# Attention and soft mixture of experts on one core: nine weight tiles in place of the last pair's tiles, another order at the end, and weight tiles that take the turned combine weights

## The chip, the core and the metric

The kernel runs on one core of a Trainium2 chip. The metric is the device time of one execution in microseconds. Several executions are timed and the median stands for the kernel; one further execution was profiled, and all rows of a profile in this document come from that one.

The core's engines work side by side, each through its own list of instructions: PE multiplies matrices (PEld is its weight load), DVE does vector work, ACT does activations and copies, POOL does further vector work, and SP issues the DMAs. They wait for each other by semaphores.

## The reference

An attention over 8 batches, 8 heads, 576 positions and 64 columns of a head is followed by a soft mixture of 8 experts with 4 slots each. All arrays are float32.

```python
# attention: q, k rotated (cos/sin by position), then for each head
scores = (1 / sqrt(D)) * matmul(q_rot, k_rot^T)
attn = exp(scores - max over keys); attn /= sum over keys + 1e-9
x = matmul(attn, v), written as N = 4608 rows of 512
# soft mixture of experts
logits = x @ phi                                  # 4608 x 32
d = exp(logits - max over rows); d /= sum over rows + 1e-9
slot_input = d.T @ x                              # 8 experts x 4 slots x 512
h = maximum(slot_input[e] @ w1[e], 0)             # 512 -> 1024
slot_out[e] = h @ w2[e]                           # 1024 -> 512
c = exp(logits - max over slots); c /= sum over slots + 1e-9
out = c @ slot_out                                # 4608 x 512
```

## The kernel before

**Attention.** The 64 heads are worked as 32 pairs; four pairs are a batch. A pair goes through these tasks: `load0`, `load1` bring q and k (L144); `spin` multiplies by cos and sin on POOL (L149, for pair 0 on DVE); `join` adds (L153); `high` and `low` split into two fp16 parts (L158, L162). The `m` units multiply one part and take row maxima on DVE (L184, L192); `t` units make the scores transposed (L229) and the exponentials on ACT (L230, tiles `a_t` and `a_rem`); `av` units multiply with v (L245, tile `v_in`); `o_out` copies the result to `xt` (L253). `add` sums exponential tiles on DVE into `c_t` (L260, L263), `total` adds them up on PE (L273) and `total_out` copies the sums to `s4` on ACT (L278). For most pairs the reciprocal sums then travel through DRAM (L284 to L304, tile `rb`) and POOL multiplies (L307). For the last two pairs `sums_turn` (L309) brings the sums from rows to columns on PE: five products with `fold`, a 0/1 tile of two columns, then two reciprocals that read PSUM (L316, L317); `sums_wide` (L326) spreads them, `norm_wide` (L332) multiplies. `logits` (L360), `natural` (L342, the transposes to `xn`) and the softmax over rows with a running maximum follow.

**Order.** PE, ACT, DVE, and in the attention SP and POOL too, run in the order in which the program writes the instructions. A table `WHEN` gives each task its place in a repeating beat. Ahead of the beat a start is written out: pair 0's work, the `fold` tile (L639, L641), 23 and 16 warm-up matmuls (`heat`, L630), pair 1's first tasks. After the beat the last pair's tasks are written out (L685 to L698), and then the slot inputs (L705 to L773).

**Weights.** The experts' weights come as 64 tiles of 512 KB, 32 of w1 and 32 of w2, through `load_w` (L477), all on SP's one queue in program order. The first 24 (pool `wp`) come during the attention. Others take memory that becomes free: `wa` and `wx` that of the q and k tiles, `wk` and `we` that of the fp16 parts, `wl` (L525, two tiles) that of `att` (`a_t`, `a_rem`, `c_t`) in `release_att`, `wb` (L767, two tiles) that of `xn`. The rest reuse `wp` tiles as FFN1 reads them out: seven issued ahead (`N_LEAD`), the others after FFN1's second group.

**The experts and the output.** FFN1 (L784) is four groups of 16 matmuls, FFN2 (L808) two halves `mh` of 16 steps of 4 matmuls. `c_turn(q)` turns a quarter of the combine weights: six transposes (`c_tr`, L448) of what `c_split` left in `csp` (an ACT copy L436 and a POOL subtraction L437), and six copies on ACT (`c_evac`, L459, L462) into `cst` and `crt`. There is one `csp`, so a split comes after the turn before it. Quarter 0 is turned between the slot inputs (L744 to L746), quarter 1 after the first FFN1 group (L858), the others where `TURNS` puts them, the last one inside the combine (L889). `gather` (L821) adds the experts' slot outputs from `so` (L812, L813); `combine` (L836, L837) multiplies and stores (L840, L843), nine stores for each half.

Of the kernel before, what the change touches and what calls it, by code (L numbers as in the profile page):

```python
# [7 lines left out]
F32 = mybir.dt.float32  # L8
F16 = mybir.dt.float16
F32R = mybir.dt.float32r  # L10
AF = mybir.ActivationFunctionType
ALU = mybir.AluOpType
AX = mybir.AxisListType
PSUM = bass.MemoryType.PSUM

B, H, S, D = 8, 8, 576, 64
HALF = D // 2
NP = H // 2
# [9 lines left out]
KB = S // D  # L28
N_W = 24
# [1 line left out]
N_WA = 5  # L31
N_WB = 2
N_WE = 3
N_WL = 2
N_X = 4
N_CS = 1
N_CE = 2
C_POOL = 4
LATE = (0, 2)
N_LEAD = 7  # L40
TURNS = (0, 0, 1, 0, 0, 0)
LEAD_STEPS = 2
STEPS = (1, 2, 2, 2, 2, 2, 2, 2, 1)
N_WARM = 23
N_CST = 4 - N_CE
RC = 12
PIECE = 4
WHEN = {
# [20 lines left out]
def attn_softmoe(ctx, tc, qk, v, phi, w1, w2, cs, ident, sel, seg, out):  # L69
    nc = tc.nc  # L70
    P = 128

    const = ctx.enter_context(tc.tile_pool(name="const", bufs=1))
    small = ctx.enter_context(tc.tile_pool(name="small", bufs=3))
    wp = ctx.enter_context(tc.tile_pool(name="wp", bufs=N_W))
# [2 lines left out]
    vals = ctx.enter_context(ExitStack())  # L78
    late = vals.enter_context(tc.tile_pool(name="late", bufs=2))
    trans = ctx.enter_context(ExitStack())  # L80
    att = trans.enter_context(tc.tile_pool(name="att", bufs=1))
    early = ctx.enter_context(ExitStack())
    stk = early.enter_context(tc.tile_pool(name="stk", bufs=4))
# [4 lines left out]
    ps_s = banks.enter_context(tc.tile_pool(name="ps_s", bufs=3, space=PSUM))  # L88
# [8 lines left out]
    id_sb = const.tile([P, P], F32, name="id_sb")  # L97
    phi_sb = const.tile([P, NP, NS], F32, name="phi_sb")
    sel_sb = const.tile([P, NS], F32, name="sel_sb")
    bits = const.tile([P, 5], F32, name="bits")  # L100
    ones, warm, tiny, fold = bits[:, 0:1], bits[:, 1:2], bits[:, 2:3], bits[:, 3:5]
    nc.vector.memset(ones, 1.0)
    lift = const.tile([P, P], F16, name="lift")
    nc.vector.memset(lift, 0.0)
# [59 lines left out]
    vts = {}  # L164

    def load_v(p):
        vts[p] = late.tile([P, KB, 2, D], F32, name="v_in")
        nc.sync.dma_start(out=vts[p], in_=v[p])

    nms = {}  # L170
# [1 line left out]
    def bank2():  # L172
        return ps_s.tile([P, 2, 512], F32, name="s_ps")
# [112 lines left out]
    rbs = {}  # L286
# [12 lines left out]

    def widen(p, eng):  # L300
        rd = sg.pop(p)
        rbs[p] = rb = late.tile([P, S], F32, name="rb", bufs=1)
        for h in range(2):
            eng.dma_start(out=rb[rows[h]], in_=rd[h:h + 1].broadcast_to([64, S]))  # L304

# [3 lines left out]
    def sums_turn(p):  # L309
        s4 = sg.pop(p)  # L310
        t = bank2()
        for j in range(5):
            w = P if j < 4 else 64
            nc.tensor.matmul(t[0:w, 0, 2 * j:2 * j + 2], lhsT=s4[:, P * j:P * j + w], rhs=fold, start=True, stop=True)
        rn = small.tile([P, RC], F32, name="rr", bufs=2)
        nc.vector.reciprocal(out=rn[:, 0:8], in_=t[:, 0, 0:8])  # L316
        nc.vector.reciprocal(out=rn[0:64, 8:10], in_=t[0:64, 0, 8:10])  # L317
        sg[p] = rn

    def sums_wide(p):  # L320
# [112 lines left out]
    def c_split(q):  # L433
        csp = c_tiles[0][2][q % N_CS]
        cb = cn_sb[:, 2 * q:2 * q + 2]
        nc.scalar.copy(out=csp[:, :, :, 0, :], in_=cb)  # L436
        (nc.gpsimd if q < C_POOL else nc.vector).tensor_tensor(  # L437
            out=csp[:, :, :, 1, :], in0=cb, in1=csp[:, :, :, 0, :], op=ALU.subtract)
# [3 lines left out]
    def c_tr(q):  # L442
        csp = c_tiles[0][2][q % N_CS]
        turning[q] = ps_s.tile([P, 2, 512], F32, name="s_ps")
        for b in range(2):
            for j in (0, 2, 4):
                w = P if j < 4 else 64
                nc.tensor.transpose(turning[q][0:w, b, 64 * j:64 * j + P],  # L448
                                    csp[:, b, j:min(j + 2, 5)].rearrange("p j a n -> p (j a n)").bitcast(F32), id_sb)

    def c_evac(q, both=False):
        cst, crt, _ = c_tiles[0]
        t = turning.pop(q)
        copies = (nc.scalar.copy, nc.vector.tensor_copy)
        for d in range(2):
            dst = slice(64 * d, 64 * d + 64)
            copy = copies[d * both]
            for s in range(2):
                copy(out=cst[q][dst, :, s::2, :],  # L459
                     in_=t[64 * s:64 * s + 64, :, 0:256].rearrange("p b (u x) -> p b u x", u=2))  # L460
                yield
            copy(out=crt[dst, 2 * q:2 * q + 2, :], in_=t[0:64, :, 320:384])  # L462
            yield

    def c_turn(q):
        c_tr(q)
        list(c_evac(q))

    w_tiles = {}
    extra = []  # L470
    later = []
    swap = list(range(4, 5 + N_CST))
    order = [n for n in range(8 * E) if n not in swap]
# [3 lines left out]
    def load_w(pool, bufs, tag="w_exp"):  # L477
        n = order[len(w_tiles)]
        layer, rest = divmod(n, 4 * E)
        if layer == 0:  # L480
            grp, f, ch, x = rest // 16, rest // 8 % 2, rest // 4 % 2, rest % 4
            src = w1[4 * grp + x].rearrange("(c p) f -> p c f", p=P)[:, 2 * ch:2 * ch + 2, 512 * f:512 * f + 512]
            wt = pool.tile([P, 2, 512], F32, name=tag, bufs=bufs)
        else:
            mh, grp, fh, x = rest // 16, rest // 8 % 2, rest // 4 % 2, rest % 4
            src = w2[4 * grp + x].rearrange("(c p) m -> p c m", p=P)[:, 4 * fh:4 * fh + 4, 256 * mh:256 * mh + 256]
            wt = pool.tile([P, 4, 256], F32, name=tag, bufs=bufs)
        nc.sync.dma_start(out=wt, in_=src)
        w_tiles[n] = wt
# [22 lines left out]
    def release_att():  # L512
        trans.close()
        cp = ctx.enter_context(tc.tile_pool(name="cp", bufs=1, side="right", reuse_waits="tile"))
        cst = [cp.tile([P, 2, 4, P], F32R, name=f"cst{i}") for i in range(N_CE)]
        crt = cp.tile([P, B, 64], F32R, name="crt")
        csps = [cp.tile([P, 2, 5, 2, NS], F32R, name=f"csp{i}") for i in range(N_CS)]
        c_tiles.append((cst, crt, csps))
        extra.append([cp.tile([P, 2, 2, 256], F32R, name=f"so{i}") for i in range(2)])
        seg_in = cp.tile([P, 320], F32, name="seg_in")  # L520
        nc.sync.dma_start(out=seg_in, in_=seg)
        seg_sb = cp.tile([P, 320], F32R, name="seg_sb")
        nc.gpsimd.tensor_copy(out=seg_sb, in_=seg_in)
        c_tiles.append(seg_sb)
        wl = ctx.enter_context(tc.tile_pool(name="wl", bufs=N_WL, side="right", reuse_waits="tile"))  # L525
        for _ in range(N_WL):
            load_w(wl, N_WL)

# [107 lines left out]
    do("load1", 2)  # L636
    nc.sync.dma_start(out=phi_sb, in_=phi.rearrange("(c p) n -> p c n", p=P))
    nc.sync.dma_start(out=sel_sb, in_=sel)
    nc.vector.memset(fold, 0.0)  # L639
    for i in range(0, P, 32):  # L640
        nc.vector.tensor_copy(out=fold[i:i + 2], in_=id_sb[i:i + 2, i:i + 2])  # L641
    do("spin1", 1)
    do("spin0", 1)
    for j in range(4):
# [34 lines left out]
    p = NPAIR - 1  # L679
# [2 lines left out]
    while pending:  # L682
        step(p)
    release_stk()
    for name in ("add1", "add2", "av4", "av5", "av6", "av7", "av8", "o_out", "total", "total_out"):  # L685
        do(name, p)
    steady.close()
    release_att()
# [9 lines left out]
    natural_out([p], nc.vector.tensor_copy)  # L698
    vals.close()
    banks.close()  # L700
    ps_t = ctx.enter_context(tc.tile_pool(name="ps_t", bufs=3, space=PSUM))
    ps_a = ctx.enter_context(tc.tile_pool(name="ps_a", bufs=1, space=PSUM))
    ps_s = ctx.enter_context(tc.tile_pool(name="ps_s2", bufs=2, space=PSUM))

    eb = const.tile([P, P], F32, name="e_blk")  # L705
    e = const.tile([P, NS], F32, name="e_sel")
# [33 lines left out]
    for i in range(NP):  # L740
        nc.tensor.matmul(rp[32 * i:32 * i + 32], lhsT=dn[64:P, P + 32 * i:P + 32 * i + 32],
                         rhs=xn[64:P, 4, i * P:(i + 1) * P], start=True, stop=True, tile_position=(64, 32 * i))
    mains(1)
    c_tr(0)  # L744
    c_split(1)
    list(c_evac(0))  # L746
    next(stat)
    nc.gpsimd.tensor_scalar_mul(out=zs, in0=zacc[:, 1:2], scalar1=0.25)
    nc.gpsimd.tensor_tensor(out=zs, in0=zs, in1=zacc[:, 0:1], op=ALU.add)
# [25 lines left out]
    cst, crt, _ = c_tiles[0]  # L775
# [66 lines left out]
            for h in range(2):  # L842
                nc.sync.dma_start(out=of[h::2, 512:576, ms].rearrange("b p m -> p b m"), in_=ob[64 * h:64 * h + 64])  # L843

    turned, split = 2, 2

    def c_turns(n):
        nonlocal turned, split
        for _ in range(n):
            if turned < NP:  # L850
                c_turn(turned)
                turned += 1
            if split < min(turned + N_CS, NP):
                c_split(split)
                split += 1

    prev = (0, 0, ffn1(0, 0))
    c_turn(1)  # L858
    cst.extend(extra[1].tile([P, 2, 4, P], F32R, name="w_exp", bufs=N_CST) for _ in range(N_CE, B // 2))
    c_split(2)  # L860
    split = 3
    for grp, f in ((0, 1), (1, 0), (1, 1)):
        h = ffn1(grp, f)
        ffn1_turn(*prev)
        prev = (grp, f, h)
        if (grp, f) == (0, 1):
            list(c_soft_tasks(B - 1, ps_t.tile([P, 512], F32, name="t_ps")))
            while len(w_tiles) < 8 * E:
                load_w(wp, N_W)
        c_turns(TURNS[2 * grp + f - 1])  # L870
    sos = extra[3]
    steps = ffn2_steps(0, sos[0])
    for k in range(16):
        next(steps)
# [2 lines left out]
        if k == 8:  # L877
            c_turns(TURNS[3])
    steps = ffn2_steps(1, sos[1])
    c_turns(TURNS[4])  # L880
    sl0 = gather(0, sos[0])
    c_turns(TURNS[5])
    for _ in range(LEAD_STEPS):
# [61 lines left out]
```

## Time and profile before

| what | value |
|---|---|
| timed executions | 596.29, 599.23, 595.2 us; median 596.29 |
| the profiled execution | 591.94 us, of which the span of the records is 590.2 us |
| PE busy | 529.8 us, 90% of the span |
| DVE, ACT, POOL busy | 430.9, 330.1, 296.6 us |
| HBM read, written | 99.93 MB, 9.58 MB |
| mean granted clock of TensorE | 0.974 |
| first FFN1 matmul (L784) | at 518.75 us |
| first store issued (L840), last two (L843) | 556.23 us, from 581.45 us on |

A row of a view with a time in front gives start and duration in us, engine, line, operation, tile written and tiles read, shapes and the count of records; in brackets the idle time of the engine before it and what ended that. A float32 matmul leaves two records. A row of the waits gives who waited for whom, us in total, times and the longest.

### The profile page before, as it was taken

The numbers are of one execution on the slowest core, as the hardware profiler recorded it, in microseconds if no ns is written. First come the engines' busy times: TensorE is split into PE (matmuls) and PEld (weight loads), VectorE is DVE, ScalarE is ACT, GpSimd is POOL, SyncE is SP. The second block draws the span as 40 slices with busy tenths as digits, with TensorE's granted clock in tenths as the row PEclk, the third lists the DMA queues.
The fourth block names the chain that finished last, engine by engine and source line by source line (L and its number), as shares of the span: only waits on it lengthen the run. The fifth ranks groups of instructions, "written<-read, shape, count | busy, mean of one in ns | idle before, by whom it ended". The sixth has DMA issues, their size and how long they took to land.

```text
span 590.2 us, 23663 instructions
## 1 busy us (share of the span) xinstructions
PE 529.8 (90%) x10320; PEld 354.6 (60%) x10320; DVE 430.9 (73%) x644; ACT 330.1 (56%) x640; POOL 296.6 (50%) x332
## 2 busy tenths in 40 slices
PE   3569989999999999999899999999999999799870
PEld 2247667657666766667666766676667666445440
DVE  5789799789888897988878888887888742321341
ACT  2136656566757665666566666666656564453341
POOL 2756467466665655566567857657593011110000
PEclk9579999999999999999999999999999999999996
DMA  7244655555555555555655555555443246589998
GB/s 249 82 162 123 182 180 180 180 180 180 180 180 180 181 180 181 181 183 178 189 171 178 180 181 191 183 171 176 158 135 101 64 147 224 192 275 349 349 361 271
DMA packets 71735, 111.65 MB, mean 189 GB/s; under 512 B 20176, under 2 KB 47568, under 8 KB 71632
## 3 DMA queue, kind: packets, MB, share of 16 engines
q1 hardware_dynamic: 71618, 110.15, 58.0%
q8 instruction: 81, 1.33, 1.0%
q14 instruction: 22, 0.18, 0.1%
q10 hardware_dynamic: 14, 0.00, 0.0%
HBM read 99.93 MB, written 9.58 MB: 186 GB/s over the span
## 4 chain that ended last, share of the span: by engine, by line
PE 57%; DVE 15%; DMA 14%; ACT 4%; SPq 4%; issue 3%; POOL 0%; DVEq 0%; ACTq 0%; POOLq 0%
PE o_ps L245 15%; PE s_ps L229 15%; PE s_ps L273 7%; DMA rc<-s 5%; PE s_ps L182 5%; DVE nm L184 4%; DVE hl L162 4%; SPq L284 3%; DMA w_exp<-in_w 3%; PE s_ps L784 2%; DMA x_in<-in_qk 2%; PE s_ps L342 2%; DVE x_in L153 2%; DVE c_t L263 1%; PE s_ps L360 1%
## 5 line engine op out<-in xcount | busy, mean ns | idle before, releaser
L149 POOL TENSOR_TENSOR x_in<-x_in,cs_sb 128x288 f32<-128x288 f32 x248 | 221.1, 923 | 121.5 <-DMA x_in<-in_qk 116.3
L184 DVE TENSOR_REDUCE nm<-s_ps 128x2 f32<-128x576 f32 x256 | 182.3, 750 | 54.2 <-PE s_ps L182 54.0
L230 ACT ACTIVATE a_t<-s_ps 128x576 f32<-128x576 f32 x256 | 160.5, 649 | 86.9 <-PE s_ps L229 72.2
L229 PE MATMUL s_ps<-hl 64*64 64x288 f16 x3456 | 159.9, 286 | 6.7 <-ACT xn L351 5.0
L245 PE MATMUL o_ps<-a_t,v_in 64*64 64x288 f32 x2048 | 163.1, 406 | 0.6 <-ACT xt L253 0.3
L229 PEld LDWEIGHTS <-hl 64*64 64x64 f16 x3456 | 101.8, 107 | 42.8 <-issue 28.3
L182 PE MATMUL s_ps<-hl 64*64 64x288 f16 x1024 | 84.5, 296 | 18.4 <-DVE nm L184 14.4
L229 PE MATMUL s_ps<-peak,lift 64*64 64x288 f16 x1152 | 92.3, 284 | 1.5 <-DMA peak<-mr 1.2
L307 POOL TENSOR_TENSOR xt<-xt,rb 128x576 f32<-128x576 f32 x30 | 49.9, 1664 | 73.0 <-DMA rb<-r_row 73.0
L245 PEld LDWEIGHTS o_ps<-a_t,v_in 64*64 64x64 f32 x2048 | 73.1, 133 | 16.2 <-ACT xt L253 3.8
L182 PEld LDWEIGHTS <-hl 64*64 64x64 f16 x1024 | 45.6, 106 | 43.0 <-issue 26.5
L158 ACT CAST hl<-x_in 128x576 f16<-128x576 f32 (+1 forms) x66 | 43.0, 653 | 26.3 <-DVE x_in L153 24.6
L153 DVE TENSOR_TENSOR x_in<-x_in 128x1152 f32<-128x1152 f32 (+2 forms) x36 | 53.1, 1475 | 1.6 <-POOL x_in L149 1.4
L278 ACT ACTIVATE s<-s_ps,bits 128x576 f32<-128x576 f32 x32 | 23.7, 740 | 49.9 <-PE s_ps L273 29.8
L162 DVE TENSOR_TENSOR hl<-x_in,hl 128x1152 f16<-128x1152 f32 x32 | 46.6, 1458 | 1.8 <-ACT hl L158 1.8
L260 DVE TENSOR_TENSOR c_t<-a_t 128x1152 f32<-128x1152 f32 x32 | 47.1, 1472 | 0.0
L229 PEld LDWEIGHTS <-lift 64*64 64x64 f16 x1152 | 40.2, 107 | 4.6 <-issue 3.6
L273 PE MATMUL s_ps<-a_t,pick 128*32 128x288 f32 x384 | 36.7, 406 | 0.0
L253 ACT COPY xt<-o_ps 128x576 f32<-128x576 f32 x32 | 20.4, 638 | 14.0 <-PE o_ps L245 14.0
L837 DVE COPY w_exp<-t_ps 128x512 f32<-128x512 f32 x18 | 12.3, 691 | 18.5 <-PE t_ps L836 17.9
L192 DVE TENSOR_REDUCE nm<-s_ps 128x2 f32<-128x576 f32 x32 | 24.0, 751 | 1.9 <-PE s_ps L190 0.8
L263 DVE TENSOR_TENSOR c_t<-c_t,a_t 128x576 f32<-128x576 f32 x32 | 24.9, 778 | 0.1
(182 smaller groups left out, 552.1 us busy)
## 6 DMA issues: line engine op xcount, KB each, us to landing
x_in<-in_qk SPq DMA_DIRECT2D x62, 576.0 KB
w_exp<-in_w SPq DMA_DIRECT2D x63, 512.0 KB
v_in<-in_v SPq DMA_DIRECT2D x32, 576.0 KB
rb<-r_row SPq DMA_DIRECT2D x60, 144.0 KB
out<-w_exp SPq DMA_DIRECT2D x16, 512.0 KB
rc<-s SPq DMA_DIRECT2D x120, 4.5 KB
x_in<-in_qk SPq DMA_DIRECT2D x4, 288.0 KB
out<-w_exp SPq DMA_DIRECT2D x4, 256.0 KB
```

What stands on the lines that cost most here:

```text
L149: eng.tensor_tensor(out=x[:, :, c], in0=x[:, :, c], in1=cs_sb[:, :, c], op=ALU.mult)
L153: nc.vector.tensor_tensor(out=x[:, t, 0, c], in0=x[:, t, 0, c], in1=x[:, t, 1, c], op=ALU.add)
L158: nc.scalar.copy(out=halves[p][:, 1 + t, c], in_=loaded[p][:, t, 0, c])
L162: nc.vector.tensor_tensor(out=hl[:, 0:4:3], in0=x[:, :, 0], in1=hl[:, 1:3], op=ALU.subtract)
L182: nc.tensor.matmul(s[rows[c], h, 0:HC], lhsT=hl[rows[h], QH, at:at + D], rhs=hl[rows[h], KH, half[n]], start=True, stop=True)
L184: nc.vector.tensor_reduce(out=nms[p][:, n, j:8:4], in_=s[:, :, 0:HC], axis=AX.X, op=ALU.max, negate=True)
L229: nc.tensor.matmul(s[rows[h ^ n], n, 0:HC], lhsT=lhs, rhs=rhs, start=(i == 0), stop=(i == 3))
L230: nc.scalar.activation(out=weights_of(p, b).rearrange("p (n x) -> p n x", n=2), in_=s[:, :, 0:HC], func=AF.Exp, scale=SCALE)
L245: nc.tensor.matmul(o[rows[h], n, 0:HC], lhsT=vt[r, b, n], rhs=a[r, half[n]], start=(b == 0), stop=(b == KB - 1))
L260: nc.vector.tensor_tensor(out=cts[p], in0=ats[p, 0], in1=ats[p, 1], op=ALU.add)
L273: nc.tensor.matmul(s[32 * i:32 * i + 32, n, 0:HC], lhsT=pick[:, n:n + NS], rhs=parts[cut][:, half[n]], start=first, stop=last, tile_positi ...
L307: eng.tensor_tensor(out=xts[p], in0=xts[p], in1=rbs.pop(p), op=ALU.mult)
```

## The change

1. `wl` gets nine tiles instead of two. They take the place of `att` and of a new pool `vp`, which holds `v_in` (two tiles) and `rb` and closes together with `att`. Room on that side comes from `cst0`, `cst1` and the two `so` tiles, which leave the pool `cp`: all four turned combine weights and both `so` now lie in weight tiles that were read out (two in `wa`, the others in `wp`).
2. In the last pair `total` and `total_out` are written ahead of `av7`, `av8` and `o_out`.
3. `sums_turn` transposes with `id_sb` and adds on DVE (two reductions, two reciprocals in SBUF) in place of the products with `fold`. The tile `fold`, its memset and its four copies at the start are gone.
4. `c_tr(0)`, `c_split(1)` and the copies of quarter 0 are no longer ahead of FFN1, nor quarter 1 after its first group: quarter 0 is turned after FFN1's third group, quarter 1 after the fourth, quarter 2 inside FFN2's first half (after its ninth of 16 steps), quarter 3 inside the combine as before.
5. The three PSUM pools of the end get waits by tile.

At the end of SP's queue (`wk` is the load of `hx`, the next three are `we`, `seg_in` a small table) before:

```order
L488 DMA wk<-in_w 128x2x512
L488 DMA w_exp<-in_w 128x4x256 x3
L521 DMA seg_in<-in_seg 128x320
L488 DMA w_exp<-in_w 128x4x256 x2
L488 DMA w_exp_11381<-in_w 128x4x256
L488 DMA w_exp_11383<-in_w 128x4x256
L488 DMA w_exp<-in_w 128x4x256 x25
```

and now:

```order
L493 DMA wk<-in_w 128x2x512
L493 DMA w_exp<-in_w 128x4x256 x3
L525 DMA seg_in<-in_seg 128x320
L493 DMA w_exp<-in_w 128x4x256 x9
L493 DMA w_exp_11379<-in_w 128x4x256
L493 DMA w_exp_11381<-in_w 128x4x256
L493 DMA w_exp<-in_w 128x4x256 x18
```

Behind `seg_in` nine `wl` loads instead of two stand ahead of the two numbered `wb` loads; of the loads into `wp` tiles 18 are left of 25.

On PE from the last pair's `av` units to its sums (`s_11221`, now `s_11211`, is `s4`) before:

```order
L245 MATMUL o_ps<-a_t,v_in 64x288 x12
L245 MATMUL o_ps<-a_rem,v_in 64x288 x4
L273 MATMUL s_ps<-c_t,pick 32x288 x4
L273 MATMUL s_ps<-a_t,pick 32x288 x5
L273 MATMUL s_ps<-a_rem,pick 32x288
L273 MATMUL s_ps<-a_t,pick 32x288
L273 MATMUL s_ps<-a_rem,pick 32x288
L314 MATMUL s_ps<-bits,s_11221 128x2 x4
L314 MATMUL s_ps<-bits,s_11221 64x2
```

and now:

```order
L245 MATMUL o_ps<-a_t,v_in 64x288 x8
L273 MATMUL s_ps<-c_t,pick 32x288 x4
L273 MATMUL s_ps<-a_t,pick 32x288 x5
L273 MATMUL s_ps<-a_rem,pick 32x288
L273 MATMUL s_ps<-a_t,pick 32x288
L273 MATMUL s_ps<-a_rem,pick 32x288
L245 MATMUL o_ps<-a_t,v_in 64x288 x4
L245 MATMUL o_ps<-a_rem,v_in 64x288 x4
L315 MATMUL s_ps<-id_sb,s_11211 128x128 x4
L315 MATMUL s_ps<-id_sb,s_11211 64x128
```

Eight matmuls of `av7` and `av8` moved behind `total`; the turn is four transposes of 128 columns and one of 64.

On ACT in FFN1's second half and FFN2's first (L797 copies FFN1's turned result, L812 a slot output) before:

```order
L797 COPY wk<-t_ps 128x512
L459 CAST w_exp<-s_ps 64x4x128 x2
L462 CAST crt<-s_ps 64x128
L459 CAST w_exp<-s_ps 64x4x128 x2
L462 CAST crt<-s_ps 64x128
L436 CAST csp_11231<-cn_sb 128x10x32
L797 COPY wk<-t_ps 128x512
L812 CAST so_11232<-o_ps 128x256
L812 CAST so_11232<-s_ps 128x256
```

and now (L795 and L810 are these copies):

```order
L467 CAST crt<-s_ps 64x128
L441 CAST csp_11230<-cn_sb 128x10x32
L795 COPY wk<-t_ps 128x512
L810 CAST w_exp<-o_ps 128x256
L464 CAST w_exp<-s_ps 64x4x128 x2
L467 CAST crt<-s_ps 64x128
L464 CAST w_exp<-s_ps 64x4x128 x2
L467 CAST crt<-s_ps 64x128
L441 CAST csp_11230<-cn_sb 128x10x32
L810 CAST w_exp<-s_ps 128x256
```

Before, quarter 2's copies and the split after them stood ahead of FFN1's last turned copy, and the two slot-output copies followed each other; now quarter 1's copies stand in that place (their last rows are the first here), and quarter 2's copies and the last split stand between the two slot-output copies.

The diff, cut to its core:

```diff
-N_WL = 2
+N_WL = 9
-TURNS = (0, 0, 1, 0, 0, 0)
+TURNS = (0, 1, 1, 1, 0, 0)
-N_CST = 4 - N_CE
+N_CST = 2
...
+    vp = trans.enter_context(tc.tile_pool(name="vp", bufs=2))
     att = trans.enter_context(tc.tile_pool(name="att", bufs=1))
...
-        vts[p] = late.tile([P, KB, 2, D], F32, name="v_in")
+        vts[p] = vp.tile([P, KB, 2, D], F32, name="v_in")
...
-        rbs[p] = rb = late.tile([P, S], F32, name="rb", bufs=1)
+        rbs[p] = rb = vp.tile([P, S], F32, name="rb", bufs=1)
...
     def sums_turn(p):
         s4 = sg.pop(p)
         t = bank2()
+        rn = small.tile([P, RC], F32, name="rr", bufs=2)
         for j in range(5):
             w = P if j < 4 else 64
-            nc.tensor.matmul(t[0:w, 0, 2 * j:2 * j + 2], lhsT=s4[:, P * j:P * j + w], rhs=fold, start=True, stop=True)
-        rn = small.tile([P, RC], F32, name="rr", bufs=2)
-        nc.vector.reciprocal(out=rn[:, 0:8], in_=t[:, 0, 0:8])
-        nc.vector.reciprocal(out=rn[0:64, 8:10], in_=t[0:64, 0, 8:10])
+            nc.tensor.transpose(t[0:w, j // 4, P * (j % 4):P * (j % 4) + P], s4[:, P * j:P * j + w], id_sb)
+        for w, n in ((P, 4), (64, 1)):
+            k = 0 if n == 4 else 8
+            nc.vector.tensor_reduce(out=rn[0:w, k:k + 2 * n].rearrange("p (j h) -> p j h", h=2),
+                                    in_=t[0:w, k // 8, 0:P * n].rearrange("p (j i r) -> p j r i", i=4, r=32)[:, :, 0:2],
+                                    axis=AX.X, op=ALU.add)
+        nc.vector.reciprocal(out=rn[:, 0:8], in_=rn[:, 0:8])
+        nc.vector.reciprocal(out=rn[0:64, 8:10], in_=rn[0:64, 8:10])
...
-        cst = [cp.tile([P, 2, 4, P], F32R, name=f"cst{i}") for i in range(N_CE)]
+        cst = []
...
-        extra.append([cp.tile([P, 2, 2, 256], F32R, name=f"so{i}") for i in range(2)])
...
-    nc.vector.memset(fold, 0.0)
-    for i in range(0, P, 32):
-        nc.vector.tensor_copy(out=fold[i:i + 2], in_=id_sb[i:i + 2, i:i + 2])
...
-    for name in ("add1", "add2", "av4", "av5", "av6", "av7", "av8", "o_out", "total", "total_out"):
+    for name in ("add1", "add2", "av4", "av5", "av6", "total", "total_out", "av7", "av8", "o_out"):
...
-    c_tr(0)
-    c_split(1)
-    list(c_evac(0))
     next(stat)
...
-    turned, split = 2, 2
+    turned, split = 0, 1
...
     prev = (0, 0, ffn1(0, 0))
-    c_turn(1)
-    cst.extend(extra[1].tile([P, 2, 4, P], F32R, name="w_exp", bufs=N_CST) for _ in range(N_CE, B // 2))
-    c_split(2)
-    split = 3
+    cst.extend(extra[1].tile([P, 2, 4, P], F32R, name="w_exp", bufs=N_CST) for _ in range(N_CST))
...
             while len(w_tiles) < 8 * E:
                 load_w(wp, N_W)
+            cst.extend(wp.tile([P, 2, 4, P], F32R, name="w_exp", bufs=N_W) for _ in range(N_CST, NP))
+            sos = [wp.tile([P, 2, 2, 256], F32R, name="w_exp", bufs=N_W) for _ in range(2)]
...
-    sos = extra[3]
```

More of the change, by code (lines that the diff above doesn't have):

```diff
@@ L33 @@
 N_WE = 3
-N_WL = 2
+N_WL = 9
 N_X = 4
 N_CS = 1
-N_CE = 2
 C_POOL = 4
@@ L99, in attn_softmoe @@
     sel_sb = const.tile([P, NS], F32, name="sel_sb")
-    bits = const.tile([P, 5], F32, name="bits")
-    ones, warm, tiny, fold = bits[:, 0:1], bits[:, 1:2], bits[:, 2:3], bits[:, 3:5]
+    bits = const.tile([P, 3], F32, name="bits")
+    ones, warm, tiny = bits[:, 0:1], bits[:, 1:2], bits[:, 2:3]
     nc.vector.memset(ones, 1.0)
@@ L700, in attn_softmoe @@
     banks.close()
-    ps_t = ctx.enter_context(tc.tile_pool(name="ps_t", bufs=3, space=PSUM))
-    ps_a = ctx.enter_context(tc.tile_pool(name="ps_a", bufs=1, space=PSUM))
-    ps_s = ctx.enter_context(tc.tile_pool(name="ps_s2", bufs=2, space=PSUM))
+    ps_t = ctx.enter_context(tc.tile_pool(name="ps_t", bufs=3, reuse_waits="tile", space=PSUM))
+    ps_a = ctx.enter_context(tc.tile_pool(name="ps_a", bufs=1, reuse_waits="tile", space=PSUM))
+    ps_s = ctx.enter_context(tc.tile_pool(name="ps_s2", bufs=2, reuse_waits="tile", space=PSUM))
     eb = const.tile([P, P], F32, name="e_blk")
```

## The prediction

> **What bounds the kernel now.** The page's chain that ended last, read first, says who ends last over the whole span; the table of windows says it for single stages.
>
> ```profile
> PE 57%; DVE 15%; DMA 14%; ACT 4%; SPq 4%; issue 3%; POOL 0%; DVEq 0%; ACTq 0%; POOLq 0%
> 484.00:494.00 10.00, 9.67 (x224) 6.38 (x216) 3.25 (x6) 6.14 (x12) 0.60 (x2) 1.00 0.56 162
> 508.00:512.00 4.00, 2.83 (x46) 2.34 (x45) 1.06 (x4) 0.05 (x1) 1.31 (x2) 1.00 1.06 353
> 512.00:518.00 6.00, 4.54 (x56) 3.07 (x49) 4.62 (x15) 2.37 (x10) 1.62 (x6) 1.00 0.29 89
> 518.00:528.00 10.00, 9.61 (x84) 3.53 (x87) 1.68 (x3) 6.33 (x15) 1.46 (x2) 1.00 0.87 290
> 528.00:556.00 28.00, 26.54 (x304) 13.01 (x296) 7.18 (x13) 10.73 (x25) 1.78 (x3) 1.00 1.09 349
> 570.00:574.00 4.00, 3.40 (x20) 2.72 (x20) 2.83 (x5) 2.10 (x4) 0.00 (x0) 1.00 0.99 300
> 574.00:584.00 10.00, 2.20 (x12) 1.38 (x11) 2.77 (x4) 2.34 (x4) 0.00 (x0) 0.82 1.05 358
> 584.00:590.20 6.20, 0.00 (x0) 0.00 (x0) 0.00 (x0) 0.00 (x0) 0.00 (x0) 0.50 0.54 151
> ```
>
> The columns are the stretch, its length, the busy times of PE, PEld, DVE, ACT and POOL, the granted clock, the DMA share and GB/s. In the attention loop TensorE is busy for 9.67 of 10 us: there a us counts on PE alone. From 528 the DMA engines are full, at 349 GB/s. But between 512 and 528 they carry 89 and 290 GB/s. The waits and the chain of the end say what that hole costs.
>
> ```profile
> SPq L488 <- DVE xn L352: 5.8, 1, 5.8
> PE s_ps L808 <- DMA w_exp<-in_w: 2.6, 4, 0.9
> PE o_ps L808 <- DMA w_exp<-in_w: 0.9, 1, 0.9
> 554.78 8.55 DMA w_exp<-in_w
> 571.44 6.75 DMA out<-w_exp
> ```
>
> The load queue stood 5.8 us behind one wait (a weight tile that takes the place of xn). Later FFN2 stands 2.6 + 0.9 = 3.5 us for weights, the chain goes through a weight load of 8.55 us and then through an output store: the tail hangs on bytes.
>
> **The start.** The four copies into `fold` and its memset go. On DVE they stand between two instructions of the chain:
>
> ```profile
> 12.01 1.36 DVE L162 TENSOR_TENSOR hl<-x_in,hl 128x1152 f16<-128x1152 f32 x1 [0.50 <-ACT hl L158]
> 13.42 2.86 DVE L641 COPY bits<-id_sb 2x2 f32<-2x2 f32 x4
> 16.32 1.43 DVE L184 TENSOR_REDUCE nm<-s_ps 128x2 f32<-128x576 f32 x2
> 32.08 1.35 DVE L153 TENSOR_TENSOR x_in<-x_in 128x1152 f32<-128x1152 f32 x1
> 12.44 13.84 POOL L149 TENSOR_TENSOR x_in<-x_in,cs_sb 128x288 f32<-128x288 f32 x16 [10.17 <-DMA x_in<-in_qk]
> ```
>
> L184 can start when L162 ends, at 12.01 + 1.36 = 13.37 instead of 16.32: 2.95 us. What could take it back is POOL, whose 16 rotations end at 12.44 + 13.84 = 26.28; DVE joins the last of them, pair 2's, at L153, 32.08, which would move to 29.13: cover of 2.85 remains. The other taker is the clock.
>
> ```profile
> 26.00:28.00 2.00, 2.00 (x17) 1.20 (x19) 0.00 (x0) 0.67 (x1) 0.28 (x1) 0.64 0.00 0
> 34.00:36.00 2.00, 0.61 (x8) 0.37 (x9) 1.26 (x1) 1.79 (x4) 0.02 (x1) 0.57 1.00 408
> 40.00:42.00 2.00, 2.00 (x44) 1.68 (x40) 1.53 (x3) 0.65 (x1) 2.00 (x4) 0.72 0.28 113
> ```
>
> With half speed before and full speed after a switch, or the reverse, the means 0.64, 0.57 and 0.72 put the switches at 27.44 (up), 34.28 (down) and 41.12 (up), 6.84 apart. [...]
>
> [...]
>
> **Pair 30's sums.** This turn runs inside the dense loop, so its PE time counts.
>
> ```profile
> 494.00 1.26 PE L314 MATMUL s_ps<-bits,s 128*128 128x2 f32 x10
> 499.85 1.09 PE L342 MATMUL s_ps<-id_sb,xt 128*128 128x128 f32 x8
> 512.00 0.66 PE L342 MATMUL s_ps<-id_sb,xt 128*128 128x128 f32 x4
> ```
>
> The ten records of L314 take 1.26 us. Eight transposes take 1.09 and four 0.66, so one more costs 0.11 and five take 0.77: 0.5 us saved (bounds 0 and 0.5). The two new reductions on DVE are hidden: their reader comes two tasks later.
>
> **The end, up to FFN1.**
>
> ```profile
> 503.28 1.94 PE o_ps L245 x32
> 507.76 1.27 PE s_ps L314 x10
> 59.83 0.23 DVE L290 TENSOR_REDUCE rr<-rc 96x12 f32<-96x48 f32 x1 [0.35 <-DMA rc<-s]
> 516.30 0.81 PE s_ps L448 x6
> 516.78 0.59 DVE L736 SCALAR_TENSOR_TENSOR acc<-acc,al,s_ps 128x128 f32<-128x128 f32 x2
> 518.75 3.64 PE s_ps L784 x32
> ```
>
> The sums now go ahead of av7 and av8, half of L245's 1.94, 0.97; these fill PE while ACT copies the sums. The turn starts when they end, about 0.9 earlier. It takes 0.77 instead of 1.27, but two reductions stand before the reciprocals, 0.23 (L290) or a little less each, overlapped: net -0.2, bounds -0.5 and +0.2. Turning combine weights of quarter 0 (L448, 0.81) no longer stands before L762; since DVE's L736 ends only at 517.37 and the last matmuls of L762 need it, I count half of it, 0.4. FFN1 starts 0.9 + 0.2 + 0.4 = 1.5 us earlier (bounds 0.9 and 2.0). Waits by tile on the PSUM pools may add a tenth; I count 0.
>
> Against the reciprocals, which now read and write SBUF, the trace has the other ones, and a POOL instruction near them:
>
> ```profile
> L291 DVE RECIPROCAL rr<-rr x30: 223/224/225, 60.1 to 486.3; 96x12 f32<-96x12 f32 x30
> 508.13 0.86 POOL L437 TENSOR_TENSOR csp<-cn_sb,csp 128x320 fp32r<-128x320 f32 x1 [6.38 <-ACT csp L436]
> ```
>
> Thirty of them, all through the loop in which POOL rotates and normalises, stayed within 223 and 225 ns: no stall. [...]
>
> **The end, from FFN1.** Nine loads instead of two can issue when the last pair's tiles are dead, about 507. Their waits: av8 (PE) for the first, the last a_rem and c_t for the second, all done by then; behind them on SP stand only loads and stores. The two loads over xn and the seven over FFN1's tiles come after them in the queue: at 1.5 us each the nine keep SP busy to about 520, past the matmuls for which it stood. Seven more tiles of 0.524 MB at 349 GB/s are 7 x 1.50 = 10.5 us of transfer. The hole takes (349 - 89)/349 x 6 = 4.47 and (349 - 290)/349 x 10 = 1.69, so 6.16 us: it is filled, and every later byte moves 6.16 ahead.
>
> PE is the other limit. All three turns c_tr(0), (1), (2) now stand inside the FFN instead of two: +0.81. The tiles that now hold the turned weights and `so` were read by FFN1 matmuls that stand ahead of their first writers on PE: 0, and a late one would be rival B. ACT gets their copies:
>
> ```profile
> 536.66 1.17 ACT L459 CAST w_exp<-s_ps 64x512 fp32r<-64x512 f32 x2
> 539.57 0.46 ACT L436 CAST csp<-cn_sb 128x320 fp32r<-128x320 f32 x1
> 538.21 2.73 PE o_ps L808 x48
> 544.45 0.37 ACT L812 CAST so<-s_ps 128x256 fp32r<-128x256 f32 x1 [3.08 <-PE s_ps L808]
> 569.47 0.69 DVE L837 COPY w_exp<-t_ps 128x512 f32<-128x512 f32 x1 [1.08 <-PE t_ps L836]
> 570.52 10.82 SPq L840 DMA_DIRECT2D out<-w_exp  x8
> ```
>
> A turn's copies and the split after it hold ACT from 536.66 to 540.03, 3.4 us. After c_tr(2) the PE has 28 matmuls of L808 left, 56 records at 2.73/48, 3.2 us: the copy of `so` (L812) comes 0.2 late and the gather waits for it. The second half of FFN2 thus starts 1.5 - 0.81 - 0.2 = 0.5 earlier; without its 3.5 us of waiting for weights it ends 4.0 earlier. The second half's first store is ready by PE 4.0 earlier, while the bytes are 6.16 ahead. From 570 on 4 x 300 + 10 x 358 + 6.2 x 151 kB/us make 5.72 MB; stores not yet issued at 570.52 are 9 x 0.524 = 4.72: the queue then holds 1.0 MB, 2.8 us, which covers the 2.2 of lateness except for the time from issue to first byte. I let it lose about half: the end gains **5.0** (bounds 4.0 by PE, 6.16 by bytes).
>
> **Sum.** 2.95 + 0.5 + 5.0 = 8.45 us. The profiled execution of 591.94 (span 590.2) would take 583.5; the median shown is 596.29, 4.35 above it, and I keep that distance: 587.8 us. The likeliest case's own range is 585.5 to 590.5.
>
> **Rivals.**
> (A) The start's 2.95 is eaten, by POOL or by warm-up matmuls that fall in another phase of the clock: 5.5 us remain, 590.8. For it: PE at half speed in much of the first 41 us; against it: POOL's 26.28 lies before 29.13.
> (B) The end stays with PE and ACT: the three turns' copies delay FFN1's own copies and the gather by 2 us more, so that the end gains 2.5 us: 590.3. For it: 3.4 us of ACT per turn; against it: ACT is busy only 10.73 of 28 us in 528 to 556.
> (C) The change doesn't do what it says: the nine loads are freed late, after the last xt or xn, and the hole stays. Only the start, 0.5 and the 0.5 by which the second half starts earlier are left: 592.3. Against it: the tiles' last readers end before 508.
> (D) Slower: v_in, rb and the a_t tiles get other SBUF addresses, and the loop's reads meet conflicts in all 32 pairs. It cancels the gain from 8.45/32 = 0.26 us a pair; at 0.5 it gives 596.29 + 16 - 8.45 = 603.8.
>
> ```profile
> L245 PE MATMUL o_ps<-a_t,v_in x2048: 400/402/738, 38.0 to 504.3; 64*64 64x288 f32 x187
> ```
>
> Against it: these 2048 read two v_in buffers and four a_t buffers at different places, and minimum and median are 400 and 402 ns.
>
> **How the numbers follow.** Forecast 0.66, A 0.10, B 0.12, C 0.07, D 0.05. One per cent, about what a measurement tells from no change, is 5.96 us: faster means below 590.3. The forecast is nearly all faster; A and B lie about at the bound and are split; C is the same; D slower. That gives faster 0.75, same 0.20, slower 0.05. The range leaves out D and the far ends: 584.5 to 592.5.
>
> **What would show it.** Right: L184 starts near 13.4; DMA carries about 349 GB/s from 508 without a hole; FFN1 starts about 5 us earlier than 518.75; FFN2 waits for weights under 1 us; the last store lands about 8 earlier. Wrong: FFN1 early but the hole at 512 to 518 still there (C); a full DMA but gather and L812 late (B); pairs longer than before (D); a first dense matmul no earlier (A).

## The result and the profile after

The changed kernel takes 580.71 us in the median (578.42 to 581.86, four executions) where the kernel before took 597.41 on the same chip: ratio 0.9717, 95% interval 0.9669 to 0.9766. A second measurement, beside other experiments, gave 0.9791 (0.9742 to 0.984). Both say faster: 16.7 us between the first medians, 12.5 by the second ratio (14.6 between its medians, 596.58 and 582.0); the forecast was 8.45. Between the two profiled executions it is 591.94 to 580.32, 11.6 us; the spans are 590.2 and 578.5.

The start, in the chain of the changed kernel (start, length, engine, tile, line, count):

```profile
13.28 3.99 DVE nm L184 x6
34.10 1.18 PE s_ps L229 x15
490.55 0.70 PE s_ps L315 x5
```

The first row maximum starts at 13.28 instead of 16.32. The five transposes of pair 30 (L315) take 0.70 where L314 took 1.26. The table of windows at the end (columns as before):

```profile
504.00:508.00 4.00, 2.70 (x42) 2.08 (x42) 1.93 (x7) 0.24 (x2) 0.17 (x1) 1.00 1.02 337
508.00:512.00 4.00, 2.77 (x31) 1.24 (x31) 3.06 (x11) 1.38 (x8) 2.47 (x7) 1.00 1.09 352
512.00:518.00 6.00, 5.62 (x38) 2.07 (x41) 0.88 (x4) 0.00 (x0) 0.00 (x0) 0.72 1.09 348
518.00:528.00 10.00, 10.00 (x92) 3.74 (x88) 2.91 (x6) 2.10 (x6) 0.92 (x2) 1.00 1.10 349
560.00:570.00 10.00, 5.77 (x31) 4.29 (x30) 5.90 (x9) 4.85 (x9) 0.00 (x0) 0.90 1.05 345
```

The hole is gone: 348 and 349 GB/s where 89 and 290 stood. New is the clock of 0.72 in 512 to 518. The chain of the end, after the change:

```profile
513.42 8.69 PE s_ps L782 x64
543.15 1.00 PE o_ps L806 x16
558.66 0.38 ACT kl L822
561.60 6.37 DMA out<-w_exp
```

FFN1 (L782) starts at 513.42 instead of 518.75, FFN2's second half at 543.15 (before: 545.65, the row below), and the second gather's copy `kl` comes at 558.66. The same marks before the change:

```profile
545.65 1.07 PE L808 MATMUL o_ps<-w_exp 128*32 128x256 f32 x16
568.27 0.38 ACT kl L824
```

So FFN2's second half up to `kl` took 22.6 us and takes 15.5. The waits of PEld, the weight load of TensorE, say why. Before:

```profile
PEld s_ps L808 <- DMA w_exp<-in_w: 4.6, 4, 1.4
PEld o_ps L808 <- DMA w_exp<-in_w: 1.9, 3, 1.4
```

and after the change the only one left on a weight transfer:

```profile
PEld s_ps L782 <- DMA w_exp<-in_w: 0.3, 1, 0.3
```

The rows of PE had shown 3.5 us; those of PEld show 4.6 + 1.9 = 6.5. The profile's end of a matmul is modelled, and here it reaches into the wait behind it:

```profile
551.63 0.62 PE L808 MATMUL o_ps<-w_exp 128*32 128x256 f32 x2 [0.90 <-DMA w_exp<-in_w]
```

Two records alone are given 0.62 us where sixteen in a row (the row at 545.65) take 1.07. So two records just before a wait cover the first half us of it: the wait in this row is 0.90 on PE and 1.38 on PEld. The 7.1 us by which the stage got shorter lie near PEld's 6.5, not near 3.5.

### The profile page after: what moved, and what is told of

It is laid out like the page before. It is cut to its first block, busy times and chain, and to the rows that moved or that the text cites. A ratio compares the mean times of both kernels' runs of the same rounds, so it can differ in the third digit from the quotient of the medians.

```text
span 578.5 us, 23626 instructions
## 1 busy us (share of the span) xinstructions
PE 527.7 (91%) x10310; PEld 353.2 (61%) x10310; DVE 426.9 (74%) x643; ACT 330.7 (57%) x640; POOL 286.6 (50%) x332
## 3 DMA queue, kind: packets, MB, share of 16 engines
q8 instruction: 81, 1.33, 0.9%
## 4 chain that ended last, share of the span: by engine, by line
PE 63%; DVE 12%; DMA 11%; ACT 6%; SPq 3%; issue 3%; POOL 0%; DVEq 0%; ACTq 0%
PE o_ps L245 17%; PE s_ps L229 17%; PE s_ps L273 7%; PE s_ps L182 5%; DMA rc<-s 4%; DVE nm L184 4%; DMA x_in<-in_qk 3%; SPq L284 3%; DVE hl L162 3%; PE s_ps L347 2%; PE s_ps L782 2%; DMA r_row<-rr 2%; PE s_ps L365 2%; ACT xn L356 1%; DVE x_in L153 1%
## 5 line engine op out<-in xcount | busy, mean ns | idle before, releaser
L149 POOL TENSOR_TENSOR x_in<-x_in,cs_sb 128x288 f32<-128x288 f32 x248 | 214.9, 899 | 130.8 <-DMA x_in<-in_qk 115.9
L245 PE MATMUL o_ps<-a_t,v_in 64*64 64x288 f32 x2048 | 163.6, 407 | 0.7 <-ACT xt L253 0.3
L245 PEld LDWEIGHTS o_ps<-a_t,v_in 64*64 64x64 f32 x2048 | 72.9, 133 | 17.1 <-ACT xt L253 4.5
L158 ACT CAST hl<-x_in 128x576 f16<-128x576 f32 (+1 forms) x66 | 43.1, 655 | 24.4 <-DVE x_in L153 22.6
L153 DVE TENSOR_TENSOR x_in<-x_in 128x1152 f32<-128x1152 f32 (+2 forms) x36 | 54.6, 1517 | 2.7 <-POOL x_in L149 2.2
L162 DVE TENSOR_TENSOR hl<-x_in,hl 128x1152 f16<-128x1152 f32 x32 | 44.7, 1398 | 1.8 <-ACT hl L158 1.8
L273 PEld LDWEIGHTS s_ps<-a_t,pick 128*32 128x32 f32 x384 | 16.4, 110 | 14.3
```

Source lines behind the costliest of these rows:

```text
L149: eng.tensor_tensor(out=x[:, :, c], in0=x[:, :, c], in1=cs_sb[:, :, c], op=ALU.mult)
L153: nc.vector.tensor_tensor(out=x[:, t, 0, c], in0=x[:, t, 0, c], in1=x[:, t, 1, c], op=ALU.add)
L158: nc.scalar.copy(out=halves[p][:, 1 + t, c], in_=loaded[p][:, t, 0, c])
L162: nc.vector.tensor_tensor(out=hl[:, 0:4:3], in0=x[:, :, 0], in1=hl[:, 1:3], op=ALU.subtract)
L245: nc.tensor.matmul(o[rows[h], n, 0:HC], lhsT=vt[r, b, n], rhs=a[r, half[n]], start=(b == 0), stop=(b == KB - 1))
L273: nc.tensor.matmul(s[32 * i:32 * i + 32, n, 0:HC], lhsT=pick[:, n:n + NS], rhs=parts[cut][:, half[n]], start=first, stop=last, tile_positi ...
```

## The experiments

The ratios are to the kernel before, measured beside it; the profile of each is one execution.

**before_again**: the kernel before, unchanged.

> The kernel before once more, unchanged. Theory: single executions of it spread over 592 to 599 us, the profiled one of 591.94 lay at the low end, and the surplus of the others is spread over the attention loop (pair 31's sums, copied at 506.96 there, come 3 to 7 us later in a slower execution, the end after them takes the same 83 us). Rival: the surplus lies in the end stage (the weight loads), then the copy of pair 31's sums stays at 507 and the stage behind it is longer. Ratio to the kernel before 1.000 within 0.005 by both.

Ratio 1.0005 (0.9963 to 1.0046). Its times went from 590.25 us, at a mean granted clock of 0.976, to 599.73; those around 599 have 0.955 to 0.961. The profiled one has a span of 592.8. Its windows before FFN1, and then FFN1 and `kl` in its chain:

```profile
510.00:514.00 4.00, 3.14 (x41) 2.36 (x35) 1.54 (x4) 0.13 (x1) 0.45 (x1) 0.57 0.95 314
514.00:518.00 4.00, 2.65 (x21) 0.91 (x19) 2.39 (x8) 1.46 (x8) 1.36 (x5) 0.50 0.04 12
518.00:521.00 3.00, 3.00 (x22) 2.02 (x19) 1.28 (x5) 0.25 (x1) 0.00 (x0) 0.53 0.09 22
```

```profile
522.43 3.64 PE s_ps L784 x32
571.77 0.38 ACT kl L824
```

In the execution of the prediction the clock was 1.00 in all three. Here it is half from 510.6 to 520.8 (from the means 0.57 and 0.53); FFN1 starts at 522.43, 3.7 later, and `kl` is 3.5 later, although the copy of pair 31's sums lies at 507.34, only 0.4 later. My theory on record put the surplus into the attention loop: in this execution it falls. The rival, the end stage, holds, and what differs there is the clock. But this span is only 2.6 longer than that of the prediction's execution; none of those around 599 was profiled. These 10.2 us at half speed lower the mean clock by 0.009 (half of 10.2 us, of 590), and it reaches 0.955, so by this estimate the slowest ones have more such time, where isn't known.

**sums_only**: the third part of the change alone, in the kernel before.

```diff
-    bits = const.tile([P, 5], F32, name="bits")
+    bits = const.tile([P, 3], F32, name="bits")
...
-    nc.vector.memset(fold, 0.0)
-    for i in range(0, P, 32):
-        nc.vector.tensor_copy(out=fold[i:i + 2], in_=id_sb[i:i + 2, i:i + 2])
```

with the changed `sums_turn`.

> The kernel before with the third part alone: sums turned by transposes, the tile fold and its copies gone. Theory of the prediction: the first row maximum 2.95 us earlier, the whole 3.5 us faster, ratio 0.994 (0.993 to 0.996). Rival A (the start is eaten by POOL or by the phase of the clock): ratio 0.999 to 1.000, with the first dense matmul no earlier. Rival, a part of the unforecast gain hangs on the start (another phase of the loop): ratio under 0.990.

Ratio 0.9886 (0.9832 to 0.9939), 6.8 us. That is the third case, more than the 3.5 of the theory. Its mean clock over the timed executions is 0.973, that of before_again 0.963.

**copies_back**: the changed kernel with the start's copies.

```diff
+    nc.vector.memset(fold, 0.0)
+    for i in range(0, P, 32):
+        nc.vector.tensor_copy(out=fold[i:i + 2], in_=id_sb[i:i + 2, i:i + 2])
     do("spin1", 1)
```

> The changed kernel with the memset and the four 2x2 copies put back at the start, into columns that nothing reads. Theory: 2.95 us slower than the changed kernel, ratio to the kernel before about 0.977. Rival A: no slower than the changed kernel, ratio 0.972. Rival of the unforecast gain from the start: more than 5 us slower, ratio 0.981 or more.

Ratio 0.9818 (0.9762 to 0.9874). Taken as written this is the last case, above 0.981. But its bounds were set from the first ratio, 0.972, and beside the kernel before measured with it even late_loads (below, which turned out to be the change itself in another order) has 0.9768. Against that it is 3.0 us, as forecast. The intervals overlap, so the times alone don't decide.

**late_loads**: two of the nine loads where the change has them, seven written behind the others.

```diff
-        for _ in range(N_WL):
+        for _ in range(2):
             load_w(wl, N_WL)
+        extra.append(wl)
...
     for _ in range(N_LEAD):
         load_w(wp, N_W)
+    for _ in range(N_WL - 2):
+        load_w(extra[-1], N_WL)
```

> The changed kernel with only two of the nine loads where the change issues them; the other seven come in the queue behind the two over xn and the seven over FFN1's tiles, so both holes of the transfers are back. Theory (the end is bound by bytes): 6.2 us slower than the changed kernel, ratio about 0.982, and FFN2 waits for weights again. Rival (the end follows PE, as the prediction's lower bound): 3 to 4 us slower. Rival C (the loads' place does nothing): same time, 0.972.

Ratio 0.9768 (0.9713 to 0.9822): no slower. It doesn't test the question: behind the attention SP's order isn't held to the program's, and three of the seven loads stood ahead of the two over `xn` again. SP waited 0.5 us for `xn`, and the transfers ran at 340 to 356 GB/s from 508 to 548.

**late_held**: the same with SP's order held until the last of these loads.

```diff
     steady.close()
+    hold = ctx.enter_context(ExitStack())
+    hold.enter_context(tc.manual_schedule(engines={mybir.EngineType.SP}))
     release_att()
```

> As late_loads, with SP's queue held to the order in which the program writes it: seven of the nine loads really stand behind the two over xn and the seven over FFN1's tiles. (In late_loads three of the seven had been put back to the front, and no hole was left.) Theory (bytes): the holes at 508 to 526 are back and it is 6 us slower than the changed kernel, more with half speed ahead of FFN1, FFN2 waiting 6 us for weights: 587 to 590. Rival (place of the loads does nothing): same time as the changed kernel.

Ratio 0.9898 (0.9866 to 0.993) beside 0.9791 of the change measured with it: 6.4 us slower. Hole and stall are back in its windows, its waits and its chain:

```profile
508.00:512.00 4.00, 2.64 (x29) 1.10 (x29) 3.06 (x11) 1.59 (x8) 2.49 (x7) 1.00 0.39 126
512.00:518.00 6.00, 5.57 (x35) 2.35 (x38) 1.16 (x5) 0.00 (x0) 0.00 (x0) 0.72 0.53 178
518.00:528.00 10.00, 10.00 (x92) 3.79 (x84) 2.91 (x6) 1.80 (x5) 0.91 (x2) 1.00 0.95 313
```

```profile
PEld s_ps L812 <- DMA w_exp<-in_w: 4.6, 4, 1.3
```

```profile
564.14 0.38 ACT kl L828
```

FFN1 starts at 513.70, as in the change, and yet `kl` comes 5.5 later. SP stands 4.7 us for `xn` and up to 5.0 for FFN1's tiles (in the change not at all and 0.5), and by the prediction's own sum the three windows lack 6.5 us of transfer at 349 GB/s. So the loads' place is worth about 6 us by itself; the intervals of the two ratios leave 3 to 10. That holding SP's order costs nothing of its own was not tested apart.

**after_again**: the changed kernel.

> The changed kernel once more, beside the three next ones. Both theories: ratio to the kernel before 0.972 to 0.977 (580 to 582 us where before has 595 to 597). Theory (bytes hide the clock): its times spread over about 3 us, less than the 9 us of the kernel before, though one stretch of half speed ahead of FFN1 shows in the profile.

Ratio 0.9791 (0.9742 to 0.984), a little above the 0.972 to 0.977 of both theories, 580.0 to 584.01 us. That is a spread of 4 us in six executions, where the kernel before had 589 to 599.8 in 23 beside it. The spread alone proves little: after_warm, whose mean clock is 0.973 to 0.976, and order_back below have 6 and 7 us. In this profiled execution the clock did not drop ahead of FFN1 (1.00 from 504 to 526); the first two groups took 7.07 instead of 8.69 us, and the span is 579.5, no less than 578.5.

```profile
514.09 7.07 PE s_ps L782 x64
557.77 0.38 ACT kl L822
559.78 6.58 DMA out<-w_exp
```

**before_warm** and **after_warm**: small matmuls in TensorE's waits ahead of FFN1.

```diff
+    def keep(out, n):
+        for i in range(n):
+            nc.tensor.matmul(out, lhsT=lift, rhs=peaks[0][:, 0:HC], start=True, stop=True)
...
+    ow = ps_o.tile([P, 2, 512], F32, name="o_ps")[:, 0, 0:HC]
+    keep(ow, 10)
     sums_turn(p)
+    keep(ow, 4)
     sums_wide(p)
+    keep(ow, 6)
```

and so on up to FFN1 (the first ten not in after_warm).

> The kernel before with 35 small idle matmuls (128 x 288, fp16, about 0.12 us each, nothing reads their result) in the waits of TensorE between the last pair's sums and FFN1, so that the clock has no reason to drop there. Theory (the distance of 4 to 5 us between the profiled execution and the others is half speed between 508 and 520, which delays FFN1 and the weight loads that wait for it): 591 us or less, ratio 0.990 to 0.993, mean granted clock 0.972 or more in all executions. Rival (the distance has another cause): ratio 1.000, or above it by the 0.5 us that the added matmuls cost.

> The changed kernel with 25 such matmuls in the same waits. Theory (from 504 on the end hangs on bytes, not on PE): FFN1 runs at full speed, 1.5 us shorter, and the time stays within 0.5 us of the changed kernel. Rival (the end still hangs on PE): 1.5 us faster.

before_warm: ratio 0.9949 (0.9914 to 0.9984), median 591.47 beside 596.58; mean clock 0.973 over its executions, 0.962 over those of the kernel before. By the ratio that is 3.0 us (1.0 to 5.1), by the medians 5.1; the ratio falls short of the theory's 0.990 to 0.993. Two of its twelve executions still took 595.4 and 595.8, at 0.972, so not all of the spread goes by the mean clock. Its windows:

```profile
510.00:514.00 4.00, 3.98 (x53) 2.77 (x51) 1.71 (x7) 0.10 (x1) 0.45 (x1) 1.00 0.99 333
514.00:518.00 4.00, 3.15 (x37) 1.59 (x37) 2.47 (x9) 1.49 (x8) 1.36 (x5) 1.00 0.07 22
```

The clock holds, the hole stays (22 GB/s). So this clock is worth 3 us of the distance between 591.94 and the median, which is 5.5 in the result; the rest is open within the interval. after_warm: ratio 0.9792 (0.9737 to 0.9847) beside 0.9791: nothing. Its clock is 1.00 in these windows, `kl` comes at 556.98, and the span is 579.1, where the change with one stretch at half speed had 578.5: after the change the end hides such a stretch.

**sums_only_warm** and **copies_late_warm**: the third part, and the start alone, on top of before_warm.

```diff
     heat(16)
     join(1, 0)
+    nc.vector.memset(fold, 0.0)
+    for i in range(0, P, 32):
+        nc.vector.tensor_copy(out=fold[i:i + 2], in_=id_sb[i:i + 2, i:i + 2])
```

(and these lines removed above, in copies_late_warm).

> sums_only with the added idle matmuls of before_warm. Theory (of the 7.0 us of sums_only 3.5 are start and sums, the rest is that its clock dropped for fewer windows ahead of FFN1): 3.5 us faster than before_warm and within 1 us of sums_only, 588. Rival (sums_only won 7 by its own work): 7 us faster than before_warm, 584.5.

> before_warm (which holds the clock ahead of FFN1) with the memset and the four copies into fold moved behind the warm-up matmuls, where DVE waits for them: the start term by itself. Theory: 2.95 us faster than before_warm, 588.5. Rival A: not faster than before_warm, 591.5.

sums_only_warm: 0.9888 (0.9841 to 0.9934), the same as sums_only; against before_warm, 0.9888/0.9949, 3.7 us. That is the theory's value: by it 3.5 are its own work, and the rest of sums_only's 6.8 is clock. Both ratios together leave 0.2 to 7.1, though, so the rival's 7 is not excluded. copies_late_warm: 0.9932 (0.989 to 0.9974), against before_warm only 1.0 us, with intervals of 2.5 us either way: the times don't decide. Its profile does: the first maximum is at 13.29,

```profile
13.29 3.12 DVE nm L184 x5
```

and over all profiled executions the copy of pair 30's sums lies at 493.09, 493.46, 493.72 and 491.18 with the copies at the start, and at 488.14 to 491.05 (ten executions, mean 489.6) without: 3.2 us between the means, with single executions up to 1.5 off. In the changed kernel alone, where only copies_back has the copies, it is 491.18 against a mean of 489.6 over seven, 1.6; in the kernel before 3.7.

**order_back**: the last pair's old order.

```diff
-    for name in ("add1", "add2", "av4", "av5", "av6", "total", "total_out", "av7", "av8", "o_out"):
+    for name in ("add1", "add2", "av4", "av5", "av6", "av7", "av8", "o_out", "total", "total_out"):
```

> The changed kernel with the last pair's tasks in the old order (av7, av8 and the output copy ahead of the sums). Theory (the end hangs on bytes, whose loads wait for av8): within 0.7 us of the changed kernel, either way, though FFN1 starts 0.9 us later. Rival (the prediction's PE chain counts): 0.9 us slower.

Ratio 0.9786 (0.9733 to 0.9839): within 0.3 us of the 0.9791 of after_again, though the intervals are 3 us either way. The traces are finer: from the copy of pair 30's sums FFN1 starts 24.7 later here and 23.9 later in the change, so the order brings 0.8 there; the span ends 88.5 later here and 88.9 later in the change (89.3 in after_again). What the second part brings at FFN1 doesn't reach the end.

**few_bytes**: four weight loads less; FFN2's second half reads the four tiles before them twice instead.

```diff
-            while len(w_tiles) < 8 * E:
+            while len(w_tiles) < 8 * E - 4:
                 load_w(wp, N_W)
+            for n in range(8 * E - 4, 8 * E):
+                w_tiles[n] = w_tiles[n - 4]
```

> The changed kernel without the last four weight loads (the second half of FFN2 uses the four tiles before them twice, so its result is another), 2.1 MB or 6.0 us of transfer less, PE's work the same. Theory (bytes alone set the end): 6 us faster than the changed kernel. Rival (PE's chain to the second gather, at 557.8 to 558.7 now, lies just under the bytes): 1 to 2 us faster only.

Ratio 0.98 (0.9747 to 0.9853): nothing, against the 6 us of the theory. In its windows the transfers now have gaps, and in its chain `kl` comes when it came before:

```profile
540.00:550.00 10.00, 9.78 (x118) 5.64 (x114) 3.25 (x6) 5.69 (x13) 0.86 (x1) 1.00 0.87 285
560.00:564.00 4.00, 3.28 (x19) 2.60 (x19) 3.17 (x6) 2.80 (x6) 0.00 (x0) 1.00 0.93 240
```

```profile
514.91 7.07 PE s_ps L782 x64
558.51 0.38 ACT kl L822
```

and from FFN1 to the end of the span (578.7) it is 63.8 us, beside 65.1 in the change and 65.4 in after_again. So after the change bytes and PE are within 2 us of each other, and the bytes alone no longer set the end.

## Why the prediction was wrong

**The start**, forecast 2.95: right. The maximum moved by 3.04, pair 30's sums by 3.2 in the mean of the profiled executions, copies_back lost 3.0 by its ratio. The times alone would leave room for rival A's zero; the marks in the traces don't. Between the two traces of the result the lead at pair 30's sums is 3.53, within the loop's scatter of a us.

**Pair 30's sums**, 0.5: right (1.26 to 0.70).

**FFN1's earlier start**, 1.5 beyond the first two terms: right in size. 518.75 - 513.42 = 5.33, of which 4.0 stand in the lead at the transposes of pairs 29 and 30 before (499.92 to 495.90), so 1.3. The order's share of it is 0.8 (order_back), forecast 0.9, and the end doesn't feel that share. The last pair's reciprocals, now in SBUF, took 0.20 and 0.10 us at 503.91; no POOL instruction ran beside them (the next is at 507.82), so what one would cost them was not shown.

**The hole**, 6.16 us of transfer: right. In 60 us (from 512 before, from 508 after) the transfers run at 318 and 354 GB/s, 2.16 MB or 6.2 us more; late_held puts it at 6.4 by the ratio.

**"Without its 3.5 us of waiting for weights it ends 4.0 earlier"**: this term was mis-sized. The wait was 6.5 us on PEld, and the stage got 7.1 shorter. FFN2's second half started 2.5 us earlier, not 3.95: FFN1's first groups at half speed took 1.6 of it (8.69 instead of 7.07). Even so PE comes to `kl` 9.6 earlier, not 7.5. So PE did not hold the bytes back as I reckoned, and "I let it lose about half" cost the sum another us: from the transposes at 499.92 to the end of the span the gain is 11.7 - 4.0 = 7.7 us, beyond both my bounds for the end (4.0 and 6.16); the hole gives 6.2 of it. The remaining 1.5 lies behind those 60 us, in the last stores: against 349 GB/s the last 18.2 us before lose 3.6 (280 GB/s) and the last 10.5 after lose 2.2 (277). In after_again such a stretch loses 3.0, so this rest isn't steady, and its cause is open. No run undoes the fourth and fifth parts alone, so their share in the 7.7 is open too. Terms put right: 3.5 + 0.5 + 7.7 = 11.7, the difference of the spans. With the distance kept that gives 596.29 - 11.7 = 584.6, still 3.9 above what was measured.

**"The median shown is 596.29, 4.35 above it, and I keep that distance"**: this step failed. The profiled execution of the kernel before happened to keep full speed ahead of FFN1. The other profiled one started FFN1 3.7 us later for it, and holding the clock made the kernel 3.0 us faster (1.0 to 5.1). In the changed kernel the loads no longer wait for these matmuls, one stretch at half speed hides under the transfers (after is 1.6 us slower than after_again in FFN1, and its span is 1.0 shorter), and its profiled execution, 580.32, lies 0.4 under its median. So the 3.0 us that before_warm wins were a cost of the kernel before, not an offset of the measurement. In numbers: 11.6 between the profiled executions, plus 5.5 from 591.94 to the median before, less 0.4 from 580.32 to the median after, make the 16.7 between the medians. In the second measurement the part beyond 11.6 is 0.9 by the ratio and 3.0 by the medians, so the size of this step depends on the executions that were drawn.

A row of the kernel before hinted at it. In the first of these two stretches TensorE is busy for only 1.95 of 4 us, though the clock held in this execution (in before_warm, where it held too, for 3.98):

```profile
510.00:514.00 4.00, 1.95 (x34) 1.34 (x31) 2.44 (x6) 1.08 (x6) 0.68 (x2) 1.00 0.90 294
514.00:518.00 4.00, 3.73 (x44) 2.47 (x44) 3.00 (x11) 1.29 (x5) 1.40 (x6) 1.00 0.07 13
```

What decides in which execution the clock drops there was not measured; nor why the profiled execution of sums_only has only 3.4 us at half speed there (from 510.8), that of before_again 10.2.

Of the rivals B, C and D none came: `kl` is early, the hole is gone, and L245 has 402 ns in the median as before. B's mechanism is there in small. In the changed kernel's chain the turn of quarter 1 (L453) waits 0.25 us (0.5 on PEld) for the split that follows quarter 0's copies (L442):

```profile
531.21 0.88 POOL csp L442
532.13 0.88 PE s_ps L453 x6
```

## What to carry to other kernels

Where one profiled execution lies outside the spread of the timed ones, ask which cost it escaped before carrying the distance over. The mean granted clock of each execution is a first hint. Read a stall of TensorE on the weight load's rows too, since matmul ends are modelled: here 6.5 us stood there and 3.5 on the matmuls. When a load queue no longer waits for compute, it also stops paying for what makes that compute late, here FFN1's 1.6 us at half speed.

## What the runs showed of the hardware

Ahead of FFN1 TensorE's granted clock drops to 0.5 in some of the profiled executions, for 3.4 us (from 513.3 in the changed kernel, where FFN1's first two groups take 8.69 us instead of the 7.07 of after_again) or for 10.2 us (from 510.6 in before_again). In others of the same two kernels it stays at 1.00 (the prediction's execution, after_again). The busy share alone doesn't tell them apart. In the 3.4 us ahead of the drop TensorE is busy 2.17 us in before_again and 2.81 in the changed kernel; in the prediction's execution, whose clock held, two stretches of this length, from 506.4 and 509.8, have 2.15 and 2.10. With 35 added matmuls whose results nobody reads (the first ten took 1.33 us) it stayed at 1.00 in the profiled execution of before_warm, and that kernel was 3.0 us faster by the ratio (1.0 to 5.1), although FFN1 started later there (520.63 instead of 518.75).
